# Value tiles of the early groups loaded in their used rows, and a new instruction order at the front, in a fused attention and two-mixture kernel

## The chip, the cores and the metric

The kernel runs on one core of a Trainium2 chip. The metric is the device time of one launch in microseconds (us), as the median of several runs. The engines are TensorE (PE: matmuls; PEld: its weight loads), VectorE (DVE), ScalarE (ACT), GpSimd (POOL) and SyncE (SP, which issues most transfers). Each engine takes its own instructions strictly in the order in which the program issues them.

## The reference

Attention with a sparse mask, then a dense two-layer network (relu squared), then one of 8 small experts per token:

```
q, k, v: (4, 8, 576, 64)
scores = q @ k.T / 8
heads 0-3: 0 <= query - key < 32
heads 4-7: query >= key and query = key mod 32
attn = softmax(masked scores) @ v           -> x (2304, 512)
h = relu(x @ w_in); y = (s * h * h + b) @ w_out       (512 -> 2048 -> 512)
e = argmax(y @ w_gate); out = gate * sigmoid gate * (relu(y @ w1[e]) @ w2[e])
```

## The kernel before

The attention is cut into 23 groups (`GROUPS`), called g0 to g22 here. A group of kind "L" holds the local heads of 2 to 4 blocks of 64 queries, with 96 keys per block. Kinds "P" and "T" hold the strided heads, the first and the later queries of a batch. The first nine groups (`NEARLY = 9`) are loaded by `load_qkv` as two tiles each: queries and keys (k = 0), then values (k = 1), 128 partitions high. A value tile of a local group has data that is read in 96 of its rows, one of a "T" group of batch 0 in 108, one of a "P" group in 128.

`attn(g)` then does, for one group:

1. mask (L632, L634) and scores (L639) on PE, into a pair of PSUM banks;
2. row maximum (L650, DVE), negated scale (L653, ACT), exp (L658, ACT, one instruction per head and block), sums and reciprocal (L672, L673, DVE), normalisation (L675, DVE);
3. transposes (L695, PE) and their copy out of PSUM (L701, ACT);
4. the product with the values (L725, PE) and its copy out of PSUM (L756 or L758 into `x0` for unit 0; L762 and L766 into `xsl` for the others).

The 2304 tokens are cut into five units (256, 512, 512, 512, 512). Unit 0 is filled by g0, g1 and g2; g2 gives two copies, one per PSUM bank. While attention goes on, `moe1` runs the first layer (L1091) for unit 0 on seven 128-wide pieces of the hidden layer, held back in `gw`, and then the second layer of all seven (L1125). Both use full float32 weights `wf`, which DVE puts together from the 64-bit input by three instructions each (L987, L990, L993, `split_w64`). After that the split arithmetic of the large units begins (L1095).

The order on every engine is made when the program is built. Each piece of work is a generator that yields `op(...)`: the engines it could use with an estimated duration, the events and tokens it waits for, and a penalty. `Order.run` always takes the piece with the least start plus priority. Two rules put dummy matmuls into PE's order: `warm` (L2380) as long as unit 0 is not complete, and `filler` (L2393) wherever the planner expects PE to be idle by 0.5 us or more in this part. Dummies read zeros, and their results are not used. Estimates thus never change what is computed, only the order on the engines and the number of dummies.

The early second layer takes four PSUM banks that attention has used so far; its first matmul waits until the last reader of the first of these banks is done.

Of the kernel before, what the change touches and what calls it, by code (L numbers as in the profile page):

```python
# [9 lines left out]
AF = mybir.ActivationFunctionType  # L10
ALU = mybir.AluOpType
# [3 lines left out]
DVE = mybir.EngineType.DVE  # L15
# [21 lines left out]
P = 128  # L37
# [12 lines left out]
NEARLY = 9  # L50
# [18 lines left out]
P_INDEX = 0.15  # L69
P_INDEX_PE = -0.3  # L70
P_EVAC = 1.5
P_SQ = -0.3
P_NORM = 0.0
P_ATT1 = -0.1
# [8 lines left out]
P_STREAM = -0.2  # L83
P_OPS = 0.1
PACE = dict(zip(range(9, 23), (0, 0, 0, 0, 0, 0, 0, 0, 0, 0, 0, 0, 0, 0)))
SCRATCH = 4096
CUT, CUT1 = 7, 12
NGATE = 2 * CUT
# [5 lines left out]
def steps():  # L94
# [6 lines left out]
GROUPS = [("L", 0, 0, 2), ("L", 0, 2, 2), ("P", 0, 0, 4),  # L101
# [10 lines left out]
def part_of(g):  # L112

    kind, b = GROUPS[g][0:2]
    late = kind == "T"
    if g >= NEARLY:
        return FIRST[b] * late, CLS if late else FIRST[b], 2 if late else QG // FIRST[b]
    return FIRST[b] * late, CLS if late else FIRST[b], RES[b][late]


def dims(g):

    if GROUPS[g][0] == "L":
        return (QB, LK) if g < NEARLY else (QG, 2 * QG)
    j0, j1, r = part_of(g)
    if g >= NEARLY:
        return r * (j1 - j0), r * j1
    return r * (j1 - j0), QB if GROUPS[g][0] == "P" else r * j1
# [67 lines left out]


LAT = 0.25
DMA_LAT = 1.8
LATE_LAT = 0.8  # L200
PH_LAT = 0.8
# [14 lines left out]
class Order:  # L216
# [14 lines left out]
    def spawn(self, gen, prio=0.0, after=True, pe=None):  # L231
        st = [self.fin + LAT if after else 0.0, prio, self.count, gen, None, prio if pe is None else pe]
        self.count += 1
        self.resume(st)
# [11 lines left out]
    def set(self, ev, t=None):  # L246
        ev.t = self.fin + LAT if t is None else t

    def free(self, tok, t=None):
        tok.free.append(self.fin + LAT if t is None else t)  # L250

    def look(self, st):
# [26 lines left out]
        for e, d, *pen in engs:  # L279
# [3 lines left out]
            for key in keys:  # L283
                for x, y in self.last.get(key, {}).items():
                    if x != e:
                        a = max(a, y + LAT)
            end = a + d + sum(pen)
# [5 lines left out]
    def run(self):  # L293
        while self.streams:
# [16 lines left out]
            for key in keys:  # L311
                self.last.setdefault(key, {})[e] = self.fin
            st[0] = self.fin + LAT
            self.resume(st)


def op(*engs, waits=(), dep=True, on=(), late=0.0):
    return engs, waits, dep, on, late
# [6 lines left out]
def body(ctx, tc, qkv, w12, moe_s, moe_b, wg, e12, out):  # L325
    nc = tc.nc
# [10 lines left out]
    at = at_ctx.enter_context(tc.tile_pool(name="at", bufs=2))  # L337
# [58 lines left out]
    t_w, t_l1 = Tok(2 * NF), Tok(2)  # L396
# [67 lines left out]
    t_qe, t_qk, t_vv, t_pt, t_ph = Tok(NQE), Tok(1), Tok(1), Tok(1), Tok(1)  # L464
# [99 lines left out]
    ev_qkv = {x: Ev() for x in LOADS}  # L564
# [7 lines left out]
    xuses = []  # L572
# [9 lines left out]
    def load_qkv(at):  # L582
        g, k = LOADS[at]
        w = widths(g)[k]
        yield op(("DMA", 0.00128 * w + (1.2 if at == 2 else 0.0)), waits=([t_qe] * (k == 0) + [t_w] if g < NEARLY else [(t_qk, t_vv)[k]]),
                 late=LATE_Q[at] if at < len(LATE_Q) else P_QKL)
        if g < NEARLY:
            t = wp.tile([P, w], F32, name="qkv", tag="w")
        else:
            t = at_pool.tile([P, (WQ, WV)[k]], F32, name="qkv", tag=("qk", "vv")[k], bufs=1)[:, 0:w]  # L590
        wq = widths(g)[0]
        nc.sync.dma_start(out=t, in_=qkv[g, k * P * wq:P * (wq + k * w)].rearrange("(p n) -> p n", n=w))
        qkvs[g, k] = t
        o.set(ev_qkv[g, k], o.fin + DMA_LAT + (LATE_LAT if g >= NEARLY else 0.0))
        step = 2 if g >= NEARLY else 1
        if at + step < len(LOADS):
            o.spawn(load_qkv(at + step), after=False)
        if g < NEARLY <= LOADS[at + 1][0]:
            o.spawn(load_qkv(at + 2), after=False)

    def attn(g):
        kind, b, i0, n = GROUPS[g]
        strided = kind == "P"
# [3 lines left out]
        qw, w = dims(g)  # L607
# [3 lines left out]
        pairs = pair_early  # L611
        singles = t_att + t_l2
# [7 lines left out]
        pr, pr_tok = buf("pr")  # L620
        pr = pr[:, 0:2 * n * w].rearrange("p (h i k) -> p h i k", h=2, k=w)
# [5 lines left out]
        k = qk[:, nqk:].rearrange("p (a t) -> p a t", a=2)  # L627
# [18 lines left out]
        cols = m * w  # L646
        v = [sm[:, a:a + m] for a in (0, 8, 16)]
        bc = [x.rearrange("p (h i) -> p h i", h=2).unsqueeze(3).to_broadcast([P, 2, n, w]) for x in v]
        yield op(("DVE", cols / 960 + 0.16), on=toks)
        nc.vector.tensor_reduce(out=v[0].rearrange("p (h i) -> p h i", h=2), in_=sc, axis=AX.X, op=ALU.max)  # L650
        if g in EXPB:
            yield op(("ACT", 0.22))
            nc.scalar.activation(out=v[2], in_=v[0], func=AF.Copy, scale=-0.125)  # L653
            for h in range(2):
                for i in range(n):
                    j = h * n + i
# [14 lines left out]
        yield op(("DVE", 0.35))  # L671
        nc.vector.tensor_scalar(out=v[1], in0=v[1], scalar1=1e-9, scalar2=None, op0=ALU.add)  # L672
        nc.vector.reciprocal(out=v[2], in_=v[1])  # L673
        yield op(("DVE", cols / 960 + 0.15))
        nc.vector.tensor_tensor(out=pr, in0=pr, in1=bc[2], op=ALU.mult)  # L675
        o.free(t_sm)
        nj = n // 2 if strided else n
        halves = [(singles if 2 * nj <= 4 else pairs, (0, 1))]
        for some, hs in halves:
# [16 lines left out]
            if 1 in hs:  # L696
                o.free(pr_tok)
            yield op(("ACT", nt * P / 1200 + 0.19), ("DVE", nt * P / 960 + 0.12, P_EVAC), on=toks)
            dst = ph[0:nk, hs[0]:hs[-1] + 1]
# [7 lines left out]
        tot = sum(nq)  # L707
        segs = segments("L" if local else "S", *span(g))
        deps = [ev_l1[u] for u in sorted(set().union(*(x[3] for x in segs)))]
        yield op(("PE", 0.245 * n + 0.1 if strided else 0.34 + 0.18 * n), waits=[pairs if strided else singles, ev_qkv[g, 1]] + deps)  # L710
        toks = [t for t in o.got if t in t_att or t in t_l2]
        vv = qkvs.pop((g, 1))
        ogs = banks_of(toks)
        rows = 2 if strided else 1
        nb = n // rows
        for j in range(nb):
            for p in range(2):
                for h in range(2):
                    for r in range(rows):
                        i, a = r * nb + j, r * QB  # L720
# [25 lines left out]
                a = t0 - b * S - i0 * QB  # L746
                runs.append((toks[0], 2 * m, src[:, :, a:a + m], [xk["L"][:, :, hl, c:c + m] for hl in range(2)], k == len(segs) - 1))
        for k, (tok, nn, src, dst, done) in enumerate(runs):
            yield op(("ACT", nn / 1200 + 0.2), ("DVE", nn / 960 + 0.15, P_EVAC), on=[tok])
            if xuses[g] == {0}:  # L750
                t0, t1 = span(g)
                dst = x0[:, 0:2, t0:t1]
                if not local:
                    dst = x0[:, 2:4, t0:t1].rearrange("q a (j r) -> q a j r", r=STRIDE)[:, :, :, r0s[k]:r0s[k] + src.shape[3]]
                if o.eng == "ACT":
                    nc.scalar.activation(out=dst, in_=src, func=AF.Copy)  # L756
                else:
                    nc.vector.tensor_copy(out=dst, in_=src)  # L758
                o.free(tok)
                continue  # L760
            if o.eng == "ACT":
                nc.scalar.activation(out=dst[0], in_=src, func=AF.Copy)  # L762
            else:
                nc.vector.tensor_copy(out=dst[0], in_=src)
            yield op(("DVE", nn / 960 + 0.15), on=[tok])
            nc.vector.tensor_sub(out=dst[1], in0=src, in1=dst[0].bitcast(F32))  # L766
            if done:
                o.free(tok)
# [12 lines left out]
    def late_waits(g):  # L781
        return [ev_qkv[g, 0], ev_ml, t_sm, t_pr[g % NPR]] + ([ev_k[PACE[g]]] if g in PACE else [])

# [48 lines left out]
    def late_rest(g, sm, ps4):  # L832
# [30 lines left out]
        for x in range(2):  # L863
            for y in range(nb):
                for p in range(2):
                    a, r = p * QB + x * QG, x * QB + y * QG
                    nc.sync.dma_start(out=phs[r:r + QG, p, x, 0:m * QG], in_=prt[a:a + QG, y * m * QG:(y + 1) * m * QG])
        t1 = o.fin + DMA_LAT + PH_LAT
        o.free(t_pt, t1)
# [32 lines left out]
        for z, src, dst, u in runs:  # L902
            if u == AWAY:
                yield op(("ACT", z / 1200 + 0.2), ("DVE", z / 960 + 0.15, P_EVAC), waits=[t_aw] if local or r0 == 0 else [], on=toks)
                if local:
# [12 lines left out]
                continue  # L918
            yield op(("ACT", z / 1200 + 0.2), ("DVE", z / 960 + 0.15, P_EVAC), on=toks)
            if o.eng == "ACT":  # L920
# [11 lines left out]
        for d, to, x in stores:  # L932
            yield op(("DMA", d))
            nc.sync.dma_start(out=to, in_=x)
            o.free(t_aw, o.fin + DMA_LAT)
        if stores:
# [8 lines left out]
    def load_w64(at):  # L945
# [5 lines left out]
        raw64[j] = t  # L951
        o.set(ev_r[j], o.fin + DMA_LAT)
        if at == 12:
# [84 lines left out]
    def chain(k, u, h, ev, box):  # L1038
# [6 lines left out]
        if held:  # L1045
# [4 lines left out]
            to = gt[:, 0:U]  # L1050
        yield op(("DVE", U / 960 + 0.15), ("ACT", U / 1200 + 0.19, P_SQ))
        if o.eng == "DVE":
# [159 lines left out]
    def make_sums(q):  # L1212
# [15 lines left out]
        nc.sync.dma_start(out=sd[q][:, 2, :], in_=a21)  # L1228
        t1 = o.fin + DMA_LAT
        o.set(ev_sd[q], t1 + 0.5)  # L1230
# [10 lines left out]
    def stream(u):  # L1241
        for q in range(NF // 2):
# [3 lines left out]
            ev = Ev()  # L1246
            o.set(ev, o.fin + DMA_LAT + 0.3)
            to = s_place(q)
# [247 lines left out]
    def put_aside(u):  # L1496
# [5 lines left out]
        for c in range(KD):  # L1502
            yield op(("ACT", U / 1200 + 0.2), ("DVE", U / 960 + 0.15, P_EVAC), waits=[t_x1] if c == 0 else [], dep=(c == 0))
            if c == 0:
# [19 lines left out]
    def finish(u):  # L1524
# [7 lines left out]
        for c in range(KD):  # L1532
            if add:
# [7 lines left out]
                continue  # L1541
            yield op(("ACT", U / 1200 + 0.2), ("DVE", U / 960 + 0.15, P_EVAC), waits=[t_x1] if c == 0 else [], dep=(c == 0))
            if c == 0:
# [871 lines left out]
    n = nc.values_load(ex["li"][0:1, 1:2], min_val=0, max_val=NTAB, skip_runtime_bounds_check_because=why)  # L2415
# [94 lines left out]
```

## Time and profile before

| | |
|---|---|
| median of 3 runs | 662.09 us (661.8 to 662.46) |
| the profiled execution, its own time | 662.37 us |
| its span in the trace | 660.6 us |
| PE busy | 651.9 us, 99% of the span |
| DVE busy | 426.6 us, 65% |
| ACT busy | 312.8 us, 47% |
| transfers | 83.81 MB, mean 127 GB/s |

The span is the time between the first and last recorded work; the 1.8 us between it and the execution's time lie around it. "Busy" of PE counts modelled ends, so that neighbouring matmuls overlap in the record; the start of the next row says better when a row is over. An idle time in brackets stands before the row, with what ended it.

### The profile page before, as it was taken

To read this page: it belongs to the slowest core of one execution; us is meant where nothing else is said; L and a number is where in the kernel's file an instruction comes from. 1 tells how busy PE (TensorE), PEld (TensorE's weight loads), DVE (VectorE), ACT (ScalarE), POOL (GpSimd) and SP (SyncE) were. 2 spreads that over 40 slices of the span, in tenths; PEclk is the share of its full clock that TensorE was granted. 3 is DMA by queue.
4 is the path that set the end of the run, shared out by engine and by line. 5 is a ranking of instruction groups with operands and counts; after the bars stand their busy time and mean duration, and the time that the engine had idled before them with its cause. 6 is when DMAs were issued, how large, how long until landed. Compare 5 with 4: busy or idle time off the path is not lost. (4 is left out here: it accounts for less than half of the span.)

```text
span 660.6 us, 14155 instructions
## 1 busy us (share of the span) xinstructions
PE 651.9 (99%) x5424; PEld 570.0 (86%) x5424; DVE 426.6 (65%) x1001; ACT 312.8 (47%) x848; POOL 38.8 (6%) x135
## 2 busy tenths in 40 slices
PE   7999999999999999999999999999999999999997
PEld 6888888899878888898899889988899999998996
DVE  5898868776545557566575767887687566535540
ACT  4876865677566444353243464543322423314311
POOL 7650000000000000000000000000000000000000
PEclk9999999999999999999999999999999999999999
DMA  8982356673544232112211242333220660910201
GB/s 312 405 334 96 112 209 208 207 245 103 177 152 169 81 106 65 49 48 97 87 50 42 64 152 68 116 97 96 96 65 2 177 237 14 327 44 16 81 1 66
DMA packets 40823, 83.81 MB, mean 127 GB/s; under 512 B 6701, under 2 KB 20142, under 8 KB 39986
## 3 DMA queue, kind: packets, MB, share of 16 engines
q1 hardware_dynamic: 40658, 82.87, 37.2%
q8 instruction: 43, 0.70, 0.5%
q14 instruction: 26, 0.21, 0.1%
q0 software_dynamic: 96, 0.02, 0.0%
HBM read 64.11 MB, written 15.63 MB: 121 GB/s over the span
## 5 line engine op out<-in xcount | busy, mean ns | idle before, releaser
L1095 PE MATMUL h<-xsl,w 128*128 128x512 f32 (+1 forms) x492 | 109.5, 369 | 0.0
L1129 PE MATMUL bk<-g,w 128*128 128x512 f32 (+1 forms) x480 | 105.5, 368 | 0.0
L1190 PE MATMUL bk<-g,w 128*128 128x512 f32 x396 | 102.2, 393 | 0.0
L1095 PEld LDWEIGHTS h<-xsl,w 128*128 128x128 f32 x492 | 84.8, 188 | 15.6 <-issue 0.4
L1968 PE MATMUL bk<-w,ht 128*128 128x512 f32 x384 | 96.0, 391 | 0.0
L1129 PEld LDWEIGHTS bk<-g,w 128*128 128x128 f32 x480 | 83.0, 188 | 14.7
L1190 PEld LDWEIGHTS bk<-g,w 128*128 128x128 f32 x396 | 69.9, 188 | 11.6
L1968 PEld LDWEIGHTS bk<-w,ht 128*128 128x128 f32 x384 | 68.6, 188 | 11.6
L1043 ACT ACTIVATE r<-h 128x512 f32<-128x512 f32 (+1 forms) x48 | 25.3, 528 | 62.5 <-PE h L1095 59.5
L1069 DVE TENSOR_TENSOR g<-r,g 128x512 fp32r<-128x512 f32 (+1 forms) x41 | 26.0, 633 | 42.6 <-ACT g L1067 42.2
L1442 PEld LDWEIGHTS h<-xsl,w 128*128 128x128 f32 x336 | 45.5, 190 | 3.8 <-issue 0.2
L1442 PE MATMUL h<-xsl,w 128*128 128x256 f32 x336 | 47.0, 283 | 0.0
L1873 ACT ACTIVATE ht<-h 128x256 fp32r<-128x256 f32 x24 | 9.2, 385 | 73.2 <-PE h L2010 47.0
L849 ACT ACTIVATE pr<-pr,sm 128x64 f32<-128x64 f32 (+2 forms) x102 | 32.8, 322 | 0.3
L1914 DVE TENSOR_TENSOR dd<-h,su 128x256 f32<-128x256 f32 x16 | 6.8, 424 | 29.5 <-PE h L2010 29.4
L1356 ACT ACTIVATE g<-dd 128x512 fp32r<-128x512 f32 x16 | 10.1, 631 | 31.5 <-DVE dd L1349 31.5
L1067 ACT ACTIVATE g<-r 128x512 fp32r<-128x512 f32 (+1 forms) x41 | 23.9, 583 | 1.7
L1055 ACT ACTIVATE r<-r 128x512 f32<-128x512 f32 (+1 forms) x41 | 23.9, 584 | 1.1
L2010 PE MATMUL bk<-x,wc 128*128 128x256 f32 x168 | 24.4, 281 | 0.0
L1442 PE MATMUL h<-xsl,s 128*128 128x256 f32 x168 | 24.3, 279 | 0.0
L1442 PEld LDWEIGHTS h<-xsl,s 128*128 128x128 f32 x168 | 22.6, 188 | 1.3
L1938 ACT ACTIVATE ob<-bk,scl 128x512 f32<-128x512 f32 x17 | 11.7, 689 | 23.5 <-PE bk L1968 22.8
(306 smaller groups left out, 1132.7 us busy)
## 6 DMA issues: line engine op xcount, KB each, us to landing
raw<-w SPq DMA_DIRECT2D x32, 512.0 KB, 6.9
qkv<-qkv SPq DMA_DIRECT2D x14, 512.0 KB, 4.7
xr<-xd SPq DMA_DIRECT2D x9, 512.0 KB, 4.7
qkv<-qkv SPq DMA_DIRECT2D x8, 544.0 KB, 6.3
out<-ob SPq DMA_DIRECT2D x17, 256.0 KB, 2.1
xd<-x SPq DMA_DIRECT2D x4, 1024.0 KB, 4.2
sraw<-sd SPq DMA_DIRECT2D x16, 256.0 KB, 2.7
wraw<-e SPq DMA_DIRECT2D x16, 256.0 KB, 3.0
```

What stands on the lines that cost most here:

```text
L849: nc.scalar.activation(out=ps4[:, h, i, :], in_=ps4[:, h, i, :], func=AF.Exp, scale=0.125, bias=v[2][:, j:j + 1], accum_out=v[1][:, j:j + 1])
L1043: nc.scalar.activation(out=r, in_=h, func=AF.Relu)
L1055: nc.scalar.activation(out=to, in_=r, func=AF.Square)
L1067: nc.scalar.activation(out=gt[:, 0, 0:U], in_=r, func=AF.Copy)
L1069: nc.vector.tensor_sub(out=gt[:, 1, 0:U], in0=r, in1=gt[:, 0, 0:U].bitcast(F32))
L1095: nc.tensor.matmul(out=h, lhsT=w_t[2 * fc][:, a, c * P:(c + 1) * P], rhs=xt(u, c, x), start=(c == 0 and n == 0), stop=(c == KD - 1 and n = ...
L1129: nc.tensor.matmul(out=acc[pu][c], lhsT=w_t[2 * pf + 1][:, a, c * P:(c + 1) * P], rhs=gt[:, x, 0:cols(pu)], start=(first and n == 0), stop ...
L1190: nc.tensor.matmul(out=acc[pu][c], lhsT=w_t[2 * pf + 1][:, a, c * P:(c + 1) * P], rhs=pbox[0][:, x, 0:cols(pu)], start=(begin and i == 0), ...
L1442: nc.tensor.matmul(out=out_, lhsT=weights(x, a, c), rhs=o_place(u, b)[y][:, c], start=(first and c == 0 and n == 0), stop=(name in ("M2", ...
L1938: nc.scalar.activation(out=ob, in_=src, func=AF.Copy, scale=scl[:, i:i + 1])
L1968: nc.tensor.matmul(out=acc2[s, t][0], lhsT=box[k][:, x, t * P:(t + 1) * P], rhs=w_t["p", 2 * f + 1][:, a, :], start=(f == 0 and n == 0), s ...
L2010: nc.tensor.matmul(out=banks[to], lhsT=t[:, a, off + c * P:off + (c + 1) * P], rhs=x2[s, b][:, y, c, :], start=(first and c == 0 and n == ...
```

## The change

Five edits. The value tiles of the local and "T" groups below g9 are loaded in their 96 or 108 used rows (`rows`). The planner's table `FRONT` gives three of the loads more time (entry 2 is the third load, entries 5 and 7 are the queries and keys of g3 and g4). The estimate of the value product of a "P" group is smaller. The copies of unit 0 out of PSUM lose DVE's penalty (`P_EV0 = 0.0`, it was 1.5), are ordered 0.6 earlier (`L_EV0`), and do not wait for one another. A variant with the normalisation on ACT is written down, but `NORM` is empty, so that it is not used.

```diff
+P_EV0 = 0.0
+L_EV0 = -0.6
...
+NORM = ()
...
+FRONT = {2: 1.8, 5: 0.5, 7: 0.3}
...
     def load_qkv(at):
         g, k = LOADS[at]
         w = widths(g)[k]
-        yield op(("DMA", 0.00128 * w + (1.2 if at == 2 else 0.0)), waits=([t_qe] * (k == 0) + [t_w] if g < NEARLY else [(t_qk, t_vv)[k]]),
+        rows = P if g >= NEARLY or not k or GROUPS[g][0] == "P" else dims(g)[1]
+        yield op(("DMA", 0.00128 * w * rows / P + FRONT.get(at, 0.0)), waits=([t_qe] * (k == 0) + [t_w] if g < NEARLY else [(t_qk, t_vv)[k]]),
                  late=LATE_Q[at] if at < len(LATE_Q) else P_QKL)
...
-        nc.sync.dma_start(out=t, in_=qkv[g, k * P * wq:P * (wq + k * w)].rearrange("(p n) -> p n", n=w))
+        nc.sync.dma_start(out=t[0:rows], in_=qkv[g, k * P * wq:P * (wq + k * w)].rearrange("(p n) -> p n", n=w)[0:rows])
...
-        yield op(("DVE", cols / 960 + 0.15))
-        nc.vector.tensor_tensor(out=pr, in0=pr, in1=bc[2], op=ALU.mult)
+        if g in NORM:
...
+        else:
+            yield op(("DVE", cols / 960 + 0.15))
+            nc.vector.tensor_tensor(out=pr, in0=pr, in1=bc[2], op=ALU.mult)
...
-        yield op(("PE", 0.245 * n + 0.1 if strided else 0.34 + 0.18 * n), waits=[pairs if strided else singles, ev_qkv[g, 1]] + deps)
+        yield op(("PE", 0.16 * n + 0.02 if strided else 0.34 + 0.18 * n), waits=[pairs if strided else singles, ev_qkv[g, 1]] + deps)
...
         for k, (tok, nn, src, dst, done) in enumerate(runs):
-            yield op(("ACT", nn / 1200 + 0.2), ("DVE", nn / 960 + 0.15, P_EVAC), on=[tok])
+            yield op(("ACT", nn / 1200 + 0.2), ("DVE", nn / 960 + 0.15, P_EV0 if xuses[g] == {0} else P_EVAC), on=[tok], dep=(k == 0 or xuses[g] != {0}), late=L_EV0 if xuses[g] == {0} else 0.0)
```

What the planner makes of it shows at two places. Line numbers of the change are 5 to 12 higher: L639 and L644 are mask and scores (L634 and L639 before), L707 and L737 the transposes and the value product (L695 and L725), L768 and L770 the copies of unit 0 on ACT and DVE (L756 and L758), L1103 and L1137 the two layers (L1091 and L1125), L2392 and L2405 the dummies (L2380 and L2393).

**First place: where unit 0 is complete.** PE before, from the end of the value product of g2 to the transposes of g3; `bk_298` and `bk_299` are the two banks of g2:

```order
L725 MATMUL bk_299<-ph,qkv 64x64
L2380 MATMUL warm<-xsl 128x256 x5
L634 MATMUL bk_442<-mh,mk 128x324 x2
L639 MATMUL bk_442<-qkv 64x108 x12
L1091 MATMUL h<-x_93,wf 128x256 x4
L695 MATMUL bk_127<-mk,pr 96x128 x6
```

and PE of the change at the same place:

```order
L737 MATMUL bk_299<-ph,qkv 64x64
L2392 MATMUL warm<-xsl 128x256
L1103 MATMUL h<-x_93,wf 128x256 x2
L639 MATMUL bk_451<-mh,mk 128x324 x2
L644 MATMUL bk_451<-qkv 64x108 x12
L1103 MATMUL h<-x_93,wf 128x256 x6
L707 MATMUL bk_127<-mk,pr 96x128 x6
```

One dummy stands where five stood, and the first layer begins ahead of the scores of g5 and has eight rows ahead of the transposes in place of four. Another single dummy stands earlier, ahead of the mask of g4. DVE before, in the same stretch (`raw_244` and the following numbers are the first weights, `bk_123` the scores of g4):

```order
L993 SCALAR_TENSOR_TENSOR wf<-raw_244,wf 128x512
L650 TENSOR_REDUCE sm<-bk_123 128x4
L990 SCALAR_TENSOR_TENSOR wf<-raw_281,wf 128x512
L987 TENSOR_SCALAR wf<-raw_328 128x512
L993 SCALAR_TENSOR_TENSOR wf<-raw_281,wf 128x512
L990 SCALAR_TENSOR_TENSOR wf<-raw_328,wf 128x512
L672 TENSOR_SCALAR sm<-sm 128x6
```

and DVE of the change:

```order
L1005 SCALAR_TENSOR_TENSOR wf<-raw_248,wf 128x512
L770 COPY x_93<-bk_299 128x16x16
L655 TENSOR_REDUCE sm<-bk_123 128x4
L1002 SCALAR_TENSOR_TENSOR wf<-raw_286,wf 128x512
L999 TENSOR_SCALAR wf<-raw_336 128x512
L1005 SCALAR_TENSOR_TENSOR wf<-raw_286,wf 128x512
L677 TENSOR_SCALAR sm<-sm 128x6
```

The copy L770 is new on DVE (it was the second L756 on ACT) and stands ahead of the row maximum of g4; the sums of g3 (L677) come one weight instruction earlier than before.

**Second place: where the early second layer begins.** PE before, from the transposes of g7:

```order
L695 MATMUL bk_803<-mk,pr 96x128 x6
L1091 MATMUL h<-x_93,wf 128x256 x4
L725 MATMUL bk_831<-ph,qkv 64x64 x12
L1091 MATMUL h<-x_93,wf 128x256 x2
L1125 MATMUL bk_937<-gw,wf 128x258
```

and PE of the change:

```order
L707 MATMUL bk_451<-mk,pr 96x128 x6
L1103 MATMUL h<-x_93,wf 128x256 x4
L737 MATMUL bk_753<-ph,qkv 64x64 x12
L2405 MATMUL bk_451<-xsl 128x256 x13
L1137 MATMUL bk_975<-gw,wf 128x258
```

The last two rows of the first layer stood between the value product of g7 and the second layer; now that layer is finished earlier, and 13 dummies stand there. The bank of the first L1137 is the one that the scores of g8 (`bk_123`) were in. ACT before, at that place:

```order
L1043 ACTIVATE r<-h 128x256
L658 ACTIVATE pr,sm<-bk_123,sm 128x64
L1055 ACTIVATE gw<-r 128x256
L658 ACTIVATE pr,sm<-bk_123,sm 128x64 x3
L762 ACTIVATE xsl<-bk_831 128x2x192
L1043 ACTIVATE r<-h 128x256
```

and ACT of the change:

```order
L1055 ACTIVATE r<-h 128x256
L663 ACTIVATE pr,sm<-bk_123,sm 128x64
L1067 ACTIVATE gw<-r 128x256
L774 ACTIVATE xsl<-bk_753 128x2x192
L663 ACTIVATE pr,sm<-bk_123,sm 128x64
```

The last exp of g8, which frees that bank, stood ahead of the copy of g7 (L762); now it stands behind it (L774).

## Rows read from the trace of the kernel before

**Rows 1.** The page: span, and PE's busy time.
```profile
span 660.6 us, 14155 instructions
PE 651.9 (99%) x5424; PEld 570.0 (86%) x5424; DVE 426.6 (65%) x1001; ACT 312.8 (47%) x848; POOL 38.8 (6%) x135
```

**Rows 2.** All waits of PE over the span: us in total, times, longest.
```profile
PE bk L639 <- DMA qkv<-qkv: 1.9, 1, 1.9
PE warm L2380 <- DVE xsl L473: 1.4, 1, 1.4
PE bk L634 <- ACT x L756: 0.3, 1, 0.3
PE bk L695 <- DVE pr L675: 0.2, 1, 0.2
```

**Rows 3.** Two stretches; at the end PEclk (granted clock), DMA share, GB/s.
```profile
11.97:13.87 1.90, 0.00 (x1) 0.00 (x0) 1.72 (x4) 0.36 (x1) 1.58 (x6) 1.00 1.02 404
...
14.90:18.10 3.20, 3.20 (x58) 2.91 (x57) 2.36 (x5) 1.95 (x8) 0.55 (x2) 0.50 1.04 412
```

**Rows 4.** PE in order of time, 9 to 21 us: start, busy us, instruction, idle.
```profile
9.15 0.61 PE L695 MATMUL bk<-mk,pr 128*96 128x128 f32 x4 [0.21 <-DVE pr L675]
...
13.87 0.73 PE L639 MATMUL bk<-qkv 64*64 64x96 f32 x24 [1.90 <-DMA qkv<-qkv]
14.53 0.89 PE L725 MATMUL bk<-ph,qkv 96*64 96x64 f32 x16
...
17.46 1.00 PE L725 MATMUL bk<-ph,qkv 64*64 64x64 f32 x32
18.40 0.86 PE L2380 MATMUL warm<-xsl 128*128 128x256 f32 x5
19.56 0.57 PE L634 MATMUL bk<-mh,mk 128*128 128x324 f32 x2 [0.30 <-ACT x L756]
20.14 0.79 PE L639 MATMUL bk<-qkv 64*64 64x108 f32 x24
```

**Rows 5.** PE's weight loads at 20.14 us.
```profile
20.14 0.58 PEld L639 LDWEIGHTS bk<-qkv 64*64 64x64 f32 x24 [0.28 <-DMA qkv<-qkv]
```

**Rows 6.** ACT in order of time: copies of unit 0, and around 43 us.
```profile
18.53 0.39 ACT L756 ACTIVATE x<-bk 128x256 f32<-128x256 f32 x1 [0.22 <-PE bk L725]
...
19.12 0.38 ACT L756 ACTIVATE x<-bk 128x256 f32<-128x256 f32 x1
...
43.39 0.33 ACT L658 ACTIVATE pr<-bk,sm 128x64 f32<-128x64 f32 x1
...
43.68 0.51 ACT L762 ACTIVATE xsl<-bk 128x384 fp32r<-128x384 f32 x1
```

**Rows 7.** DVE in order of time: a wait, and its nearest copy.
```profile
17.83 0.56 DVE L650 TENSOR_REDUCE sm<-bk 128x4 f32<-128x384 f32 x1 [0.84 <-PE bk L639]
...
30.04 0.41 DVE L766 TENSOR_TENSOR xsl<-bk,xsl 128x256 fp32r<-128x256 f32 x1
```

**Rows 8.** PE in order of time, 42 to 58 us.
```profile
42.69 0.92 PE L725 MATMUL bk<-ph,qkv 96*64 96x64 f32 x24
43.54 1.13 PE L1091 MATMUL h<-x,wf 128*128 128x256 f32 x4
44.51 2.77 PE L1125 MATMUL bk<-gw,wf 128*128 128x258 f32 x12
...
48.52 0.69 PE L725 MATMUL bk<-ph,qkv 64*64 64x60 f32 x32
49.14 8.97 PE L1125 MATMUL bk<-gw,wf 128*128 128x258 f32 x40
57.75 2.63 PE L1095 MATMUL h<-xsl,w 128*128 128x512 f32 x10
```

**Rows 9.** The only other dummies of before, and the next row.
```profile
294.57 0.76 PE L2393 MATMUL bk<-xsl 128*128 128x256 f32 x5
295.17 0.87 PE L1190 MATMUL bk<-g,w 128*128 128x512 f32 x3
```

More of the change, by code (lines that the diff above doesn't have):

```diff
@@ L673, in attn @@
         nc.vector.reciprocal(out=v[2], in_=v[1])
-        yield op(("DVE", cols / 960 + 0.15))
-        nc.vector.tensor_tensor(out=pr, in0=pr, in1=bc[2], op=ALU.mult)
+        if g in NORM:
+            for h in range(2):
+                for i in range(n):
+                    j = h * n + i
+                    yield op(("ACT", w / 1200 + 0.16), dep=(j == 0))
+                    nc.scalar.activation(out=pr[:, h, i, :], in_=pr[:, h, i, :], func=AF.Copy, scale=v[2][:, j:j + 1])
+        else:
+            yield op(("DVE", cols / 960 + 0.15))
+            nc.vector.tensor_tensor(out=pr, in0=pr, in1=bc[2], op=ALU.mult)
         o.free(t_sm)
```

## The prediction, made blind

> **What bounds the kernel now.** I read the page first: PE is busy for 651.9 of 660.6 us [rows 1]. An engine busy for 99% of the span has little to give, so the second view is the list of PE's waits: four in the whole program, 3.8 us together [rows 2]. Three of them stand in the order of time at 9.15, 13.87 and 19.56 [rows 4], the fourth ahead of the first dummies at the start. The reader is to see that after 20 us PE waits for nothing. The end of the program is therefore the moment at which PE begins the large units (L1095, 57.75 us [rows 8]) plus a remainder that keeps its length if nothing new stalls there. The third view is PE in order of time [rows 4], which shows what PE does with the first 58 us besides work: it waits 1.90 us for the queries and keys of g3, until 13.87; it runs five dummies and then idles 0.30 between 18.40 and 19.56; and part of the stretch is at half clock. [...]
>
> Since PE's real instructions are the same before and after, the change is worth what it takes away of waits, dummies and half clock ahead of L1095, less what it adds of them.
>
> **The change part by part.** *The shorter loads.* Two value tiles stand in SP's queue ahead of the load that PE waits for at 13.87, g0's and g1's, each 128 rows of 2 KB now and 96 rows then: 2 x 32 x 2 KB = 131 KB less. At the 404 GB/s that the transfers moved in that wait [rows 3] this is 0.32 us. The bounds are 0 (the time of a load does not follow its rows; there is no 96-row load in the trace) and 0.32; I take 0.3. [...]
>
> The scores of g5 waited for their load too: PE's weight loads idled 0.28 for it, until 20.14, while PE itself was still in the masks that began at 19.56 [rows 4, 5]. By then g3's value tile has saved another 98 KB. A mask and its start take 0.58 there; I count 0.1 gained, between 0 and 0.28.
>
> *The dummies ahead of g2's scores.* Six and four, on both sides of these scores, become ten ahead of them. The transposes of g0 that follow wait for DVE anyhow, with 0.21 of idle ahead of 9.15 [rows 4]. Four dummies at 0.86 / 5 = 0.17 move the scores by 0.7, into the place the later four had. Price 0; DVE's normalisation covers it, and 0.7 would be lost without that.
>
> *Unit 0's copies.* Before, the product of g2 ends at about 18.40 (the next row begins), the two copies start at 18.53 and 19.12, both on ACT with an exp between them, and PE goes on at 19.56, 0.06 after the second ends [rows 4, 6]: 1.16 us without work. In the change ACT and DVE do one copy each. A DVE copy of 256 elements out of PSUM is not in the trace; the nearest row, a subtraction of that size, has 0.41 [rows 7]; bounds 0.2 (half of it) and 0.8 (double, for the strided destination). With 0.13 to begin, perhaps 0.1 more for DVE, 0.41, and 0.06 to PE: 0.70. That is 1.16 - 0.70 = 0.46 gained, less the single dummy new ahead of g4's mask, 0.17: **0.29 gained**, with bounds of -0.1 and 0.5.
>
> This adds a wait on DVE: L770 stands in order until g2's product is over, about 18.5, and ends about 18.95. Queued behind it is the row maximum of g4, which ran at 17.83 [rows 7], so DVE is 1.1 us later from here. Who waits for that is PE's transposes of g3, through their normalisation. But PE has four more first-layer rows ahead of them now; two such rows take 44.51 - 43.54 = 0.97 [rows 8], four 1.9. So the delay is covered; without this cover 1.1 would be lost.
>
> *The first layer earlier, and 13 dummies.* The rows of the first layer that go ahead cost nothing; they are the same rows. But the last two of them stood between the value product of g7 and the second layer (43.54 to 44.51 [rows 8]), and hid the freeing of the banks. Now 13 dummies stand there. The only other dummies of this kind take 295.17 - 294.57 = 0.60 for five [rows 9], 0.12 each: 13 x 0.12 = **1.56 us lost**, and between 1.4 and 2.2 (by the slower 0.17 above). They cannot be hidden, as PE executes them in order, and PE waited for nothing there before. Is it a wait that would be there anyhow? Partly: the first L1137 needs the last exp of g8, now behind g7's copy on ACT. After the product: 0.13 to begin, about 0.25 until ACT is through with the relu, exp and square that the last first-layer step brings (three times about 0.33 and 0.1 to begin, 1.1, against the product's 0.85 [rows 6, 8]), 0.51 for the copy, 0.33 for the exp [rows 6], 0.06: 1.3 us. The 13 dummies are longer than that, so this wait costs nothing on top; without the dummies it would cost 1.3 itself.
>
> *Later on.* The late attention of g9 and g10 moves a little in PE's order past rows of the second layer and L1095. Before, PE waits for nothing there; I count 0, with no gain possible and a loss only where a wait appears. `NORM` is empty: 0.
>
> **The sum**: -0.3 - 0.1 - 0.29 + 1.56 = +0.87 us. The profiled execution took 662.37, of which 660.6 are the span, so its changed counterpart would take 663.2. It stood 0.28 above the median of 662.09, on which the forecast is made: 662.09 + 0.87 = **662.9 us** or so. A measurement of this kernel tells about 0.2% (1.3 us) from no change, so this is "same", on the slow side.
>
> **The rivals.** *B, the clock stays up.* PE's clock fell about 1 us after the long idle ended, and g2's product took 18.40 - 17.46 = 0.94 where a product of equal shape took 0.62 at full clock (48.52 to 49.14) [rows 4, 8]; a third of the 3.87 us from 14.53 to 18.40 is 1.3. With 1.6 us of idle in place of 1.9, the clock may not fall. Not all of it would be won, since a faster PE next meets the loads and DVE; between 0.5 and 1.3 I take 0.9: 662.0. For it speaks that the idle gets shorter; against it, that most of the idle is still there. [...]
>
> *C, slower: the cover at the second place is too short.* The chain through ACT has 1.56 - 1.3 = 0.26 us of slack. Every 1 us by which ACT is late there adds nearly 1 us. With 0.9 us of delay the sum is 0.87 + 0.64 = +1.5, or 663.6, and it decides from 0.7 us of delay on. For it: a chain (product, copy, exp, matmul) is exposed that before was over when the product ended, as the last exp of g8 began at 43.39, ahead of the copy at 43.68 [rows 6]. Against it: only three short instructions stand ahead of the copy on ACT.
>
> *D, the loads get no shorter.* Then 0.4 of gain is gone: 663.4, at the edge of "slower".
>
> *E, faster by more than 0.2%.* Even with B's 1.3 in full, both gains at their upper bounds (0.32, 0.28, 0.5) and the dummies at 1.4, the sum is -1.0. Only something that no row here shows would do it.
>
> **How the numbers follow.** The sum as it stands 0.50, B 0.17, C 0.15, D 0.11, E 0.07. Faster by over 0.2%: E, 0.07. Slower by over 0.2%: C, and half of D: 0.21. The rest, 0.72, is within 0.2%. The range reaches from B's 1.3 in full, less the 0.3 by which single runs lay under the median (661.4), to C with 1.5 us of ACT delay (664.2).
>
> **What would show it.** Right: PE resumes the scores of g3 at about 13.5 in place of 13.87; the first layer starts within 0.8 us of the end of g2's product; 13 dummies take about 1.6 us just ahead of L1137, which starts about 0.9 later than 44.51; L1107 starts near 58.6 (the scores of g9, 0.8 us, now stand ahead of it, so 59.4 with them). Wrong: a new wait of PE for ACT or DVE between 20 and 58 us, full clock from 14 to 18 us, or a wait after 60 us.

## The result, and the profile after

The changed kernel takes **666.56 us** (median of 6 runs, 665.95 to 667.92), against 662.28 for the kernel before (6 runs, 661.8 to 662.53): a ratio of **1.0068, interval 1.0055 to 1.0081**. It is 4.3 us slower. The forecast was 662.9 with a range of 661.4 to 664.2, so the time lies outside, on the slow side, and it is slower than any rival gave.

The page after, its span and PE's row, answers to [rows 1]. The profiled execution took 666.23 us.

```profile
span 664.5 us, 14180 instructions
PE 653.9 (98%) x5434; PEld 571.9 (86%) x5434; DVE 427.6 (64%) x1002; ACT 311.4 (47%) x847; POOL 36.8 (6%) x135
```

The list of PE's waits after (us in total, times, longest) answers to [rows 2]:

```profile
PE bk L644 <- DMA qkv<-qkv: 3.8, 3, 2.1
PE warm L2392 <- DVE xsl L477: 1.4, 1, 1.4
PE bk L707 <- DVE pr L687: 0.5, 1, 0.5
```

One wait of 1.9 us for a load has become three of 3.8 us together. The wait for DVE ahead of the transposes of g0 is 0.5 in place of 0.2. The wait for ACT's copies of unit 0 (0.3) is gone, as the change intends. PE after, in order of time, answers to [rows 4] and [rows 8]:

```profile
13.12 0.73 PE L644 MATMUL bk<-qkv 64*64 64x96 f32 x24 [0.58 <-DMA qkv<-qkv]
...
17.49 0.56 PE L644 MATMUL bk<-qkv 64*64 64x96 f32 x16 [2.08 <-DMA qkv<-qkv]
...
18.44 0.38 PE L2392 MATMUL warm<-xsl 128*128 128x256 f32 x1
18.66 1.54 PE L1103 MATMUL h<-x,wf 128*128 128x256 f32 x4
19.65 1.10 PE L639 MATMUL bk<-mh,mk 128*128 128x324 f32 x2
21.88 1.36 PE L644 MATMUL bk<-qkv 64*64 64x108 f32 x24 [1.13 <-DMA qkv<-qkv]
23.17 4.17 PE L1103 MATMUL h<-x,wf 128*128 128x256 f32 x12
27.17 0.82 PE L707 MATMUL bk<-mk,pr 128*96 128x128 f32 x6
...
46.86 1.81 PE L2405 MATMUL bk<-xsl 128*128 128x256 f32 x13
48.51 1.91 PE L1137 MATMUL bk<-gw,wf 128*128 128x258 f32 x8
...
61.95 1.14 PE L1137 MATMUL bk<-gw,wf 128*128 128x258 f32 x4
62.73 3.55 PE L1107 MATMUL h<-xsl,w 128*128 128x512 f32 x14
```

The scores of g3 start at 13.12 (before at 13.87), but those of g4 wait 2.08 us for their load and those of g5 another 1.13. The large units begin at 62.73; before they began at 57.75 [rows 8]. Some 0.8 us of that are the scores of g9 (the start of L811 at 61.16 to 61.95), which now stand ahead: 4.2 us later like for like. That is the whole loss (the two spans differ by 3.9). The list of waits has none after 62.73.

Why do the loads come later? The windows of the kernel before show at the end of each row the granted clock, the DMA share and GB/s:

```profile
15.00:20.00 5.00, 4.70 (x69) 4.00 (x67) 4.16 (x9) 3.63 (x17) 0.45 (x2) 0.67 1.03 407
20.00:30.00 10.00, 9.99 (x129) 8.00 (x132) 9.39 (x21) 7.96 (x36) 8.48 (x26) 1.00 1.03 405
...
46.00:60.00 14.00, 14.00 (x96) 11.87 (x95) 13.12 (x28) 8.57 (x18) 0.00 (x0) 1.00 0.08 33
```

and the same windows after, with four of one us each:

```profile
15.00:20.00 5.00, 2.92 (x58) 2.40 (x56) 2.72 (x6) 2.56 (x12) 3.60 (x15) 0.90 1.03 279
20.00:30.00 10.00, 8.87 (x76) 6.73 (x75) 6.80 (x15) 6.18 (x32) 5.51 (x19) 0.71 1.04 294
...
46.00:60.00 14.00, 14.00 (x122) 12.24 (x122) 13.31 (x28) 9.56 (x23) 0.00 (x0) 1.00 0.53 199
...
17.00:18.00 1.00, 0.51 (x27) 0.52 (x31) 0.00 (x0) 0.00 (x0) 0.77 (x5) 1.00 0.99 289
19.00:20.00 1.00, 1.00 (x5) 0.74 (x3) 1.00 (x3) 1.00 (x7) 0.42 (x2) 0.51 1.03 273
24.00:25.00 1.00, 1.00 (x3) 0.77 (x3) 0.97 (x4) 0.00 (x0) 0.88 (x3) 0.50 0.97 241
...
26.00:27.00 1.00, 1.00 (x7) 0.87 (x6) 1.00 (x3) 0.77 (x5) 0.90 (x2) 1.00 1.00 292
```

The share of time in which the 16 transfer engines are busy is the same, 1.03, but they move 279 GB/s in place of 407. The transfers of the front, which before were over soon after 46 us, go on behind it, though the kernel moves fewer bytes in all (83.29 MB on its page, 83.81 before). So packets have become slower, and not only those of the shortened loads, as the issues within the first 62 us show (times, KB each, median us from issue to landing), before:

```profile
raw<-w SPq DMA_DIRECT2D x18, 512.0 KB, 8.4
qkv<-qkv SPq DMA_DIRECT2D x3, 512.0 KB, 9.3
```

and after:

```profile
raw<-w SPq DMA_DIRECT2D x18, 512.0 KB, 9.6
qkv<-qkv SPq DMA_DIRECT2D x3, 512.0 KB, 11.8
```

Neither the weights `raw` nor these three loads of attention are touched by the change, and yet they land 1.2 and 2.5 us later in the median. The second thing to see in the windows after is the clock: full up to 19 us, half from 19 to 25 us, and full in 26:27. The 12 matmuls of L1103 at 23.17 are over only at 27.17.

### The profile page after: what moved, and what is told of

Read it like the earlier page. It is cut to its first block, busy times and chain, and to the rows that moved or that the text cites. A ratio compares the mean times of both kernels' runs of the same rounds, so it can differ in the third digit from the quotient of the medians.

```text
span 664.5 us, 14180 instructions
## 1 busy us (share of the span) xinstructions
PE 653.9 (98%) x5434; PEld 571.9 (86%) x5434; DVE 427.6 (64%) x1002; ACT 311.4 (47%) x847; POOL 36.8 (6%) x135
## 2 busy tenths in 40 slices
DMA packets 40615, 83.29 MB, mean 125 GB/s; under 512 B 6693, under 2 KB 20134, under 8 KB 39778
## 5 line engine op out<-in xcount | busy, mean ns | idle before, releaser
L1107 PE MATMUL h<-xsl,w 128*128 128x512 f32 (+1 forms) x492 | 109.3, 369 | 0.0
L1141 PE MATMUL bk<-g,w 128*128 128x512 f32 (+1 forms) x480 | 105.5, 368 | 0.0
L1107 PEld LDWEIGHTS h<-xsl,w 128*128 128x128 f32 x492 | 84.9, 188 | 15.5 <-issue 0.4
L1141 PEld LDWEIGHTS bk<-g,w 128*128 128x128 f32 x480 | 83.0, 188 | 14.8
```

Of the source, the lines that this page charges most:

```text
L1107: nc.tensor.matmul(out=h, lhsT=w_t[2 * fc][:, a, c * P:(c + 1) * P], rhs=xt(u, c, x), start=(c == 0 and n == 0), stop=(c == KD - 1 and n = ...
L1141: nc.tensor.matmul(out=acc[pu][c], lhsT=w_t[2 * pf + 1][:, a, c * P:(c + 1) * P], rhs=gt[:, x, 0:cols(pu)], start=(first and n == 0), stop ...
```

## The experiments

After the result there were two places for the loss: the loads in part of their rows, or the new order of the front with its dummies. Within the first there were several theories of what in such a load is slow; each expectation names the one that it tests (T, O, K, K2, P, S). P holds that every load of fewer than all 128 rows is slow, K2 that one is slow only where 16 does not divide its rows. Ratios are to the kernel before, run on the same chip, with 95% intervals.

**The new order with full loads.** The planner's estimates stay those of the change, so that the order on every engine does too; only the transfer takes all rows again.

```diff
-        nc.sync.dma_start(out=t[0:rows], in_=qkv[g, k * P * wq:P * (wq + k * w)].rearrange("(p n) -> p n", n=w)[0:rows])
+        nc.sync.dma_start(out=t, in_=qkv[g, k * P * wq:P * (wq + k * w)].rearrange("(p n) -> p n", n=w))
```

> The changed kernel with all 128 rows loaded again; the planner still counts 96 and 108, so that the order on PE, DVE and ACT is row for row that of the changed kernel. Theory T (the loads of 96 and 108 rows slow the transfers of the front; in the changed kernel these moved 305 GB/s from 20 to 40 us against 403 before): the 3.4 us beyond my sum go away, 0.87 us above before remain: about 663.2, ratio 1.001. Rival O (the new order and the 13 dummies cost it): stays near 666.5, ratio 1.006.

Measured: 663.78 us, ratio **1.0012 [1.0001, 1.0023]**. Its window from 20 to 30 us:

```profile
20.00:30.00 10.00, 9.74 (x146) 8.13 (x147) 9.02 (x20) 8.23 (x39) 7.89 (x26) 1.00 1.03 404
```

and PE in order of time:

```profile
13.20 0.73 PE L644 MATMUL bk<-qkv 64*64 64x96 f32 x24 [0.58 <-DMA qkv<-qkv]
...
16.72 0.56 PE L644 MATMUL bk<-qkv 64*64 64x96 f32 x16 [1.23 <-DMA qkv<-qkv]
...
17.89 1.03 PE L1103 MATMUL h<-x,wf 128*128 128x256 f32 x4
18.57 0.65 PE L639 MATMUL bk<-mh,mk 128*128 128x324 f32 x2
20.26 0.79 PE L644 MATMUL bk<-qkv 64*64 64x108 f32 x24 [1.03 <-DMA qkv<-qkv]
20.97 2.86 PE L1103 MATMUL h<-x,wf 128*128 128x256 f32 x12
23.67 0.82 PE L707 MATMUL bk<-mk,pr 128*96 128x128 f32 x6
...
43.36 1.81 PE L2405 MATMUL bk<-xsl 128*128 128x256 f32 x13
45.01 1.91 PE L1137 MATMUL bk<-gw,wf 128*128 128x258 f32 x8
...
59.24 4.46 PE L1107 MATMUL h<-xsl,w 128*128 128x512 f32 x18
```

The rate is back at 404 GB/s and most of the loss is gone, so it belongs to the shortened loads. Row by row the two traces say how: between this kernel and the change, the large units move from 59.24 to 62.73, 3.5 us. The scores of g4 start 17.49 - 16.72 = 0.8 later and the load of g5 costs 0.1 more of idle. The other 2.6 are half clock: what this kernel does from 17.89 to 23.67, without its wait of 1.03, takes 4.75 us, and after it takes from 18.66 to 27.17, without 1.13, 7.38. This trace also has a wait that the lists of before and of the change do not have: 0.8 us at 582 us, for weights of the experts (L2253).

**The loads alone.** The kernel before, in its own order, with the loads of 96 and 108 rows.

```diff
+        rows = P if g >= NEARLY or not k or GROUPS[g][0] == "P" else dims(g)[1]
+        nc.sync.dma_start(out=t[0:rows], in_=qkv[g, k * P * wq:P * (wq + k * w)].rearrange("(p n) -> p n", n=w)[0:rows])
```

> The kernel before, with its own order, and only the value loads in 96 and 108 rows. Theory T: slower by 2 to 4 us (the waits of PE for loads grow), 664.5 to 666. Rival O: the loads are shorter, so 662.0 or up to 0.4 less.

Measured: 666.14 us, **1.0055 [1.0039, 1.0071]**. The list of its waits begins with

```profile
PE bk L640 <- DMA qkv<-qkv: 4.2, 3, 1.8
```

in place of 1.9 in one [rows 2], at 280 to 324 GB/s between 15 and 40 us. The last of these waits is for the queries and keys of g6, which PE did not have to wait for before:

```profile
23.74 0.79 PE L639 MATMUL bk<-qkv 64*64 64x108 f32 x24
```

and with the loads alone:

```profile
26.98 0.79 PE L640 MATMUL bk<-qkv 64*64 64x108 f32 x24 [0.83 <-DMA qkv<-qkv]
```

From this row to the large units both kernels take 34.0 us (57.75 - 23.74 and 60.98 - 26.98), so the 3.2 us by which that load is waited for are the loss of this trace. The loads alone make nearly the whole loss of the change: 0.55% here and 0.12% with the order alone add up to 0.67%, against 0.68%. And here the granted clock is full in each window from 10 us on, so the half clock is not needed for it.

**Which rows? 96 alone, and 108 alone.** In the change, five of the shortened loads have 96 rows and two have 108.

```diff
+        some = rows if rows == LK else P
...
+        some = P if rows == LK else rows
+        nc.sync.dma_start(out=t[0:some], in_=qkv[g, k * P * wq:P * (wq + k * w)].rearrange("(p n) -> p n", n=w)[0:some])
```

> The changed kernel, same order; the five loads of 96 rows stay, the two of 108 rows are full again. If 108 rows alone are slow (theory K): about 663.2, as with full rows. If every partial load is slow (theory T), five sevenths of the 3.4 us stay: about 665.5. [...]

> The changed kernel, same order; the two loads of 108 rows stay, the five of 96 are full again. Theory K (108 rows alone are slow): about 666.5. Theory T: these two come at about 15 us and later in the queue, where PE waits for no load any more, so about 663.2 to 664.

Measured: 667.14 us, **1.006 [1.0045, 1.0075]** for 96 alone; 664.4 us, **1.0028 [1.0017, 1.0039]** for 108 alone. With 108 alone the rate is 408 GB/s from 15 to 20 us and falls in the stretch behind it:

```profile
20.00:30.00 10.00, 8.17 (x105) 6.64 (x106) 7.57 (x16) 7.58 (x34) 7.97 (x28) 1.00 1.04 271
```

This trace is of a run of 666.81 us; ten of the twelve runs lie between 663.61 and 665.43, so the window shows more than is usual. PE waits for loads even at 24.74 and 29.99 in it, where the expectation had none. So both counts are slow, and the five loads of 96 rows carry most of it: with them alone the kernel loses 1.6 us more than theory T's five sevenths, about as much as the whole change. Theory K, that 108 rows alone are slow, does not hold: with the loads of 96 rows alone the kernel is at 1.006. What makes either count slow no run shows.

**112 rows, and 64 and the rest.** Two other ways to leave rows out: 112 rows (seven times 16, for theory K2), and rows 0 to 63 as one load with rows 64 to 95 or 107 as another.

```diff
+        some = P if rows == P else 112
...
+        for r0, r1 in ((0, P),) if rows == P else ((0, QB), (QB, rows)):
+            nc.sync.dma_start(out=t[r0:r1], in_=qkv[g, k * P * wq:P * (wq + k * w)].rearrange("(p n) -> p n", n=w)[r0:r1])
```

> [...] Rival K2 (uneven shares are slow, even shares of 16 are fast): as e1_full_rows, 663.3.

> The changed kernel, same order, each partial value tile loaded in two pieces: rows 0 to 63, and rows 64 to 95 or 107. Theory P: slow, 665.5 to 667.5. Rival S (row counts that are no power of two are slow): the pieces of 64 and 32 are fast, only the two of 44 slow, about 663.5 to 664.

Measured: 666.99 us, **1.0064 [1.0051, 1.0076]**, and 667.05 us, **1.0065 [1.0053, 1.0077]**. Neither way helps, as theory P expected, and neither K2 nor S holds; from 20 to 30 us they move 298 and 280 GB/s.

**All bytes, in two halves.** Nothing is left out, but each of these value tiles comes as two loads of 64 rows.

```diff
+        for r0, r1 in ((0, P),) if rows == P else ((0, QB), (QB, P)):
+            nc.sync.dma_start(out=t[r0:r1], in_=qkv[g, k * P * wq:P * (wq + k * w)].rearrange("(p n) -> p n", n=w)[r0:r1])
```

> The changed kernel, same order, the seven value tiles loaded in full, but in two pieces of 64 rows each; so all the bytes of e1_full_rows in other shapes. Theory P: slow although nothing is left out, 665 to 668. Rival S: as e1_full_rows, 663.3, or up to 0.5 more for seven more issues on SP. [...]

Measured: 670.54 us, **1.0124 [1.0108, 1.0139]**, the second slowest of all. Windows:

```profile
20.00:30.00 10.00, 9.69 (x100) 7.78 (x95) 7.60 (x17) 7.13 (x35) 4.20 (x13) 0.75 1.04 289
30.00:40.00 10.00, 8.87 (x151) 7.44 (x150) 7.93 (x18) 7.60 (x36) 8.37 (x28) 1.00 1.04 266
```

With every byte loaded the rate still falls to 266 to 289 GB/s, and the time is above the 668 us that theory P allowed. The transfer engines are busy all the time (1.04), so it is not the seven more issues that slow them. What costs is that a load covers fewer than 128 rows, not what is left out. Why such loads are slow stays open: the runs show how long they and their packets take, and no cause.

The packets' own durations, worked out from the trace's packet records as a mean over the first 62 us, say how the slowness spreads (ns, by packet size):

```
                       2048 B   3072 B   4096 B
before                     97      125      168
change                    110      193      195
change, full loads         89      125      169
two halves                117      200      200
```

The 3072-byte packets are those of four of the seven value tiles, one packet a row: 125 ns with full loads, 193 to 200 in loads of fewer rows. The 4096-byte packets, 2688 in each kernel, all belong to loads that no edit touches (the weights and three loads of attention). They go from 168 and 169 to 195 and 200 ns, so loads of 128 rows beside the short ones are slowed too.

**Without the 13 dummies.** The new order with full loads, and the threshold of `filler` raised so that it puts none there.

```diff
-        if idle < (0.5 if ev_k[8].t is None else 1.2):
+        if idle < (3.0 if ev_k[8].t is None else 1.2):
```

> As e1_full_rows (all 128 rows, order of the changed kernel), without the 13 dummies ahead of the early second layer; nothing else changes. My sum has 1.56 us for them, and a wait for ACT of 1.3 us that would stand there without them: then PE idles 1.3 us in place of 1.65 and the kernel gains 0.3 us over e1_full_rows. Rival: nothing waits there, the gain is the full 1.6 us, and the kernel is 0.8 us faster than before, about 661.8.

Measured: 662.1 us, **0.9994 [0.9985, 1.0004]**. PE from the second place on:

```profile
44.05 1.98 PE L1137 MATMUL bk<-gw,wf 128*128 128x258 f32 x8 [0.95 <-issue]
...
58.35 4.45 PE L1107 MATMUL h<-xsl,w 128*128 128x512 f32 x18
```

A wait of 0.95 us stands where the 13 dummies took 45.01 - 43.36 = 1.65. The profile names nothing that ended it ("issue"); ACT's rows do: the last exp of g8 is through at 43.95, and the weight load of L1137 begins at 44.02. The dummies cost 0.7 in the traces and 1.2 by the two ratios, between the 0.3 expected and the rival's 1.6. What is left of the change without its short loads and its dummies can't be told from the kernel before.

**The other edits one by one, with full loads.** The unit 0 copies alone (they also do not wait for one another, and those dummies are left out), and the new load estimates alone. The smaller estimate for the value product of a "P" group was not run by itself.

```diff
+P_EV0 = 0.0
+L_EV0 = -0.6
...
+FRONT = {2: 1.8, 5: 0.5, 7: 0.3}
```

> The kernel before with one part of the change alone: unit 0's copies without DVE's penalty, 0.6 earlier and not waiting for one another; loads in 128 rows, estimates as before, and no dummies ahead of the early second layer (the planner would put 16 there). Two first-layer rows stay ahead of that layer as a cover. My step on the copies: 0.3 to 0.5 us gained, 661.9 to 662.2, ratio 0.9993. Rival: the part gains nothing, because PE then waits for g5's load instead (it landed at 20.14 in the kernel before): ratio 1.000.

> The kernel before with the new load estimates (FRONT) alone: loads in 128 rows, copies and other estimates as before. The planner moves dummies (ten ahead of g2's scores, three and one more before g5) and none stands ahead of the early second layer. My step: ten dummies in place of six and four cost nothing, so within 0.3 us of before, ratio 0.9997 to 1.0005. Rival: the four more dummies delay PE while it could work, plus 0.5 to 0.7.

Measured: 672.15 us, **1.0143 [1.0121, 1.0164]** for the copies; 665.87 us, **1.0055 [1.0036, 1.0073]** for the estimates. Both expectations missed. The planner makes another order of the whole front for each table, and the wait appears far behind it. The late wait with the copies alone:

```profile
PE bk L896 <- DMA phs<-prt: 3.1, 1, 3.1
```

PE in order of time with the estimates alone:

```profile
57.33 3.10 PE L1107 MATMUL h<-xsl,w 128*128 128x512 f32 x12
...
77.52 0.34 PE L896 MATMUL bk<-phs,qkv 128*64 128x64 f32 x4 [1.48 <-DMA phs<-prt]
78.14 1.04 PE L896 MATMUL bk<-phs,qkv 128*64 128x64 f32 x28 [0.28 <-DMA phs<-prt]
...
79.87 4.36 PE L1141 MATMUL bk<-g,w 128*128 128x512 f32 x12
84.07 2.90 PE L1107 MATMUL h<-xsl,w 128*128 128x512 f32 x12
```

The front is 0.4 us faster here (57.33 in place of 57.75), but the value product of a late strided group (L896) waits 1.8 us for its second operand (`phs`), which a transfer brings, and behind it 12 matmuls of L1141 take 4.36 us, at 79.87, where 12 of L1107 with operands of the same shape take 2.90 just after them. Together that is 2.9 of the 3.6 us. In the kernel before and in the change that wait does not exist. With the copies alone the same wait, 3.1 us, comes at 192 us, on top of a front that lasts until 61.51, 3.8 us longer: 6.9 of the 9.5 us; the rest was not followed up. What each edit is worth in the order of the change can't be read from these two kernels, as each has an order of its own.

**Loads earlier in the queue.** If loads end the waits of the front, the queries and keys could go ahead of the weights in SP's queue: in the kernel before, and in the new order with full loads and without the dummies.

```diff
-FIRST_LOADS = "qqqvwvwqvwqvwqvwqvwqvwqvwvw"
+FIRST_LOADS = "qqqvwvqwvqwvqwvqwvqwvqwvwvw"
```

> The kernel before with another order of its first loads: the queries and keys of g3 to g8 each one weight load (0.5 MB, 1.3 us at 404 GB/s) earlier, all in 128 rows. If PE's waits for these loads are what bounds the first 20 us (1.90 and 0.28 us in the kernel before), 1 to 2 us are gained: 660.3 to 661.5. Rival: DVE, which needs the weights, waits for them now, and nothing is gained.

> e5_no_dummies (the changed order, 128 rows, no dummies ahead of the second layer) with the loads in the same earlier order as e11. It waits for loads at three places (2.3 us in e5's profile). If these go, 1 to 2 us below e5_no_dummies: 660.3 to 661.5. Rival as in e11: no gain over e5_no_dummies.

Measured: 667.25 us, **1.0068 [1.0049, 1.0087]**, and 665.85 us, **1.0054 [1.0036, 1.0072]**. In the first the waits for loads fall from 1.9 to 1.5, but

```profile
PE bk L1125 <- DVE wf L993: 3.2, 1, 3.2
```

the second layer now waits for the last of the `wf`. It is not the load that is late: the list of DVE's waits has no load before 60 us. It begins on these weights at 48.60 (L987), then has 13 instructions of L966 for the large units in its order, 7.91 us from 49.54, and finishes `wf` only at 59.24. The trace is of a run of 665.34 us, at the lower end (665.02 to 668.07), so it does not show all of the 4.5 us lost. In the second the waits for queries and keys are down to 0.7, and the large units begin at 56.50; then the planner expects an idle time at 158 us and fills it:

```profile
158.01 2.67 PE L2405 MATMUL bk<-xsl 128*128 128x256 f32 x21
161.57 0.51 PE L1107 MATMUL h<-xsl,w 128*128 128x256 f32 x2 [0.89 <-ACT w L974]
162.30 1.45 PE L1107 MATMUL h<-xsl,w 128*128 128x256 f32 x10 [0.22 <-DVE w L978]
```

21 dummies and two waits, 162.30 - 158.01 less the 0.5 of two matmuls, are 3.8 us that the kernel before does not have there. Against a front that is 1.25 earlier that leaves 2.5 of the 3.6 us measured; the rest was not followed up. No version that was run is measurably faster than the kernel before.

## Why the prediction was wrong

**The failed step is "the shorter loads".** It took the time of a load to follow its bytes, 131 KB at 404 GB/s, or at worst not to change, and gave the bounds 0 and 0.32 us of gain. There was no bound on the side of a loss. Before, PE waits for no load after 20.14 us; in the change it waits for one until 21.88. The runs show that the loads of fewer than 128 rows are slow themselves (packets of 3072 bytes took 193 ns in place of 125) and slow others in flight beside them (packets of 4096 bytes, all of untouched loads, 195 in place of 168): 279 GB/s in place of 407 from 15 to 20 us, and 1.0055 for this edit alone. So the two terms for loads, -0.4 us together, measure about +3.6. The row for 404 GB/s [rows 3] came from loads of 128 rows, and held for none of the other shapes that were run. Rival D, "the loads get no shorter", named the place, but stopped at no gain. g5's load, the second term, came at 21.88 in place of 20.14.

One sign of the forecast came true by luck: the scores of g3 start at 13.12, near the 13.5 that the shorter loads were to give. With full loads in the same order they start at 13.20, and with the short loads in the old order at 14.14, so it is not the shorter loads that move them. What does is open.

**The rest of the sum was right in size, but partly for other reasons.** The change with full loads was to be 0.87 + 0.4 by D's terms, about 1.3 us slower; 1.0012 is 0.8 us, with an interval of 0.1 to 1.5. In its trace the large units, without the 0.8 of g9's scores, begin at 58.45, 0.7 later than before. Term by term:

*The dummies ahead of g2's scores.* Price 0 held in the end, but DVE covers only a part: the transposes of g0 start at 9.68 with full loads, 9.15 before, and DVE keeps PE idle for 0.33 ahead of them, where it was 0.21. What takes up the delay is the wait for g3's load, 0.58 in place of 1.90.

*The copies on two engines.* PE's wait for them is gone, and the first layer starts 0.2 us behind the product of g2 (18.44 to 18.66, with one dummy), where the forecast allowed 0.8. But the 0.29 is not won by it: the scores of g5 start at 20.26 with full loads and at 20.14 before, because in both it is the arrival of the queries and keys of g5 that releases them. Whatever PE wins ahead of that load goes into the wait for it. The prediction had read the load's 0.28 of idle on PEld [rows 5] and did not ask what would follow from it for gains upstream.

*The first layer earlier.* "The rows of the first layer that go ahead cost nothing; they are the same rows" gave them no credit: two of them (four matmuls) fill that wait, and so do not stand at the second place. That is worth the 0.97 of [rows 8].

*The 13 dummies.* Forecast 1.56, measured 1.65. Less 0.97 and with 0.1 for the later load, this gives 0.8, near the 0.7 that the trace shows.

*The wait for ACT without the dummies.* Forecast 1.3, measured 0.95; it was a mis-sized term, by 0.35. With it the dummies' net price is 0.7, where the prediction's two figures give 0.3.

**The rivals.** B: with full loads the clock did stay full in the profiled execution (1.00 in each window from 10 to 60 us, where before it was 0.50 from 14.90 to 18.10 [rows 3]), yet nothing was won for the reason just given: PE arrived earlier at the loads of g4 and g5 and waited 1.23 and 1.03. In the change itself it was full from 14 to 18 us too, which the prediction had named as a sign of being wrong; but the idle ahead of g4's scores grew to 2.08, and the clock fell at 19. C did not come: nothing at the second place waited for ACT beyond the dummies. *Later on*, 0, held in the change: no wait after 60 us. In the same order with full loads one of 0.8 us came at 582 us, and in the re-planned kernels of the experiments such waits decide.

## What to carry to other kernels

Loading only the used rows of a tile was no saving here: with loads of fewer than 128 rows among the others the rate of the front fell by a quarter or more in its worst window, to between 266 and 295 GB/s from 400 to 409. So load the full height, or measure such a load before costing it by its bytes. Where PE waits for a load, find out whether that load is late because of its own queue or because PE is early; in the second case no gain ahead of it reaches the end, and only work moved into the wait does. When a planner sets the order, a single constant re-plans the program, and the waits and dummies that it makes a hundred microseconds later must be read before the edit is judged.

## What the runs showed of the hardware that was not expected

- Loads of 64, 96, 108 and 112 rows were all slow. With full loads the front ran at 400 to 409 GB/s between 10 and 40 us; in each kernel that had such loads it fell to between 266 and 295 in the lowest of the windows 15:20, 20:30 and 30:40, with the transfer engines busy for the same share (1.02 to 1.05). It does not take bytes left out: two halves with all bytes were the slowest of these, at 1.0124.
- The slowness is shared. The 4096-byte packets, all of untouched loads, took 195 ns in the change and 200 with two halves, for 168 before. The time from issue to landing is a poorer sign: untouched loads of 512 KB landed 1.2 and 2.5 us later in the change, but with two halves, the slower kernel, at 8.6 and 7.9 us against 8.4 and 9.3 before.
- The granted clock after a wait is not told by the length of the wait alone. With full loads in the change's order it stayed full through waits of 0.58, 1.23 and 1.03 us, and with the loads alone through 1.51, 1.85 and 0.83; with the copies alone, waits of 1.34 and 1.15 were followed by half clock (0.50 in the windows 19:20 and 24:25), and 12 matmuls of L1103 took 4.5 us in place of 2.7. What tells these apart is open. In the trace with the estimates alone a wait of 1.8 us at 76 to 78 us was followed by a granted clock of 0.67 in 78:82.
- The granted clock in the record is not to be read in the first microseconds. With the loads alone it is 1.00 in 2:10, but 16 score matmuls at 5.39 take 0.92 us and 32 at 9.77 take 1.13, where before they took 0.56 and 0.69.
